# An attention and token-mixing kernel: the one-engine steps up to the first group's end in a written order, and strided heads of two batches on TensorE in small tiles

## The chip, the cores and the metric

The kernel runs on one core of one Trainium2 chip. The metric is the device time of one execution in microseconds, lower is better. It is given as the median of the runs shown; the profile comes from one execution of its own, whose time stands beside its span.

## The reference

The inputs are q, k, v of 8 batches, 8 heads, 576 positions and 64 features, and four weight matrices that arrive in 64-bit floats. Heads 0 to 3 attend to the last 32 positions, heads 4 to 7 to every 32nd position; the result goes through a token-mixing and a channel-mixing layer.

```python
mask_local = (rel >= 0) & (rel < 32)
mask_strided = (rel >= 0) & (pos[None, :] % 32 == pos[:, None] % 32)
scores = np.where(masks, scale * q @ k.T, -1e9)
attn = exp(scores - max); attn = attn / (attn.sum(-1) + 1e-9)
x = (attn @ v) as [batch, 576, 512]
h = np.maximum(x.T @ w_tok1, 0) @ w_tok2      # w_tok1 576 x 256, w_tok2 256 x 576
u = x + h.T
out = u + np.maximum(u @ w_ch1, 0) @ w_ch2    # w_ch1 512 x 1536, w_ch2 1536 x 512
```

## The kernel before

**Groups.** The 8 x 576 = 4608 rows of u are cut into 9 groups of 512. `mlp` handles a group: for each of 12 slices of the hidden layer `up_proj` (12 matmuls of 512 columns, line 460), a relu into gh on ScalarE (463) and the rest gl on VectorE (464), then `down_proj` (12 matmuls, 472) into four accumulators; at the group's end the output is added (486, 488) and stored (489). Every 32-bit factor is split into a high and a low part, which makes three matmuls of one.

**Batches.** Group g needs the u of batch g's main part and of the tail of batch g - 1. For a batch, `load_x` (311) reads x from two arrays in device memory, one of the local heads (xl) and one of the strided heads (xs); `tok1` splits x into xh on ScalarE (327) and xlo on VectorE (328), multiplies (336) and makes h; `tok2` transposes x into PSUM (362), adds the second layer (368), and splits into uh (370, ScalarE) and ul (371, VectorE). These steps are put between the up and down projections of the group before, at places that a table of inserts gives (`at`).

**Attention.** `local_unit` computes two local heads of a pair of batches for n chunks of 128 positions: 8n score matmuls a head pair of 64 by 32 tiles (137), a fused masked minimum on VectorE for each chunk and head (146), an exponential with its sum on ScalarE (149), transposes (160), products with v (167) and a scaling (181). The strided heads of batch 0 go through `strided_pe`: groups of 7 residues, 126 rows, in one matmul (229) with a mask that shuts 6/7 of it, transposes (244) and products (253). The strided heads of batches 1 to 7 go through `strided`: GpSimd multiplies (286, and 303 for the products with v), VectorE sums (287, 305), in 27 + 27 pieces a batch, with buffers sa, sb, and four stores to xs (307).

**Weights.** `convert` turns a raw 64-bit piece (DMA at 85, three raw buffers) into 32 bits in a buffer w_f (two of them): an absolute value on ScalarE (88), a byte copy on ScalarE (92), two steps on VectorE (93, 94). `load_split` then rounds it on ScalarE (105) and takes the rest on GpSimd (106). There are 30 such pieces: 3 of w_tok1, 3 of w_tok2, 24 of w_ch1 and w_ch2. `do_pieces` places the 24 around and inside group 0.

**Order.** Engines take instructions in a queue of their own. The program's text gives priorities, and a planner with times of its own orders each engine's queue from them; `strided` has its work 3000 places later. All DMAs are issued from SP's queue.

Of the kernel before, what the change touches and what calls it, by code (L numbers as in the profile page):

```python
# [10 lines left out]
F32 = mybir.dt.float32  # L11
# [9 lines left out]
HL = 4  # L21
# [10 lines left out]
RG = 7  # L32
RP = RG * NJ
NRG = 5
NSB = 1
FIRST = {0: 1, 4: 2}
# [4 lines left out]
SHUT = -3.0e38  # L41
TOP = 3.4e38
# [11 lines left out]
def attn_mixer_kernel(ctx, tc, qT, kT, vw, qs, ks, vs, qsT, ksT, vsP, mask, mask2, w1, w2, wt1, wt2, outT):  # L54
# [22 lines left out]


    def convert(stage, srcs, n):

# [5 lines left out]
        high = raw[:, :n, 1]  # L86

        nc.scalar.activation(out=a.bitcast(F32), in_=high.bitcast(F32), func=AF.Abs, scale=REBIAS)
# [3 lines left out]
        nc.scalar.copy(out=octets[:, :n, 4], in_=octets[:, :n, 3])  # L92
        nc.vector.tensor_scalar(out=high, in0=high, scalar1=5, scalar2=0x80000007, op0=ALU.arith_shift_right, op1=ALU.bitwise_and)  # L93
        nc.vector.scalar_tensor_tensor(out=a, in0=a, scalar=3, in1=high, op0=ALU.logical_shift_left, op1=ALU.bitwise_xor)  # L94
        return a.bitcast(F32)

    def load_split(stage, dsth, dstl, *srcs):
# [8 lines left out]
        nc.gpsimd.tensor_tensor(out=dstl, in0=f, in1=dsth.bitcast(F32), op=ALU.subtract)  # L106

    def load_t1():
        for c in range(0, NSC - 1, 2):
            load_split(stage, t1h[:, c:c + 2], t1l[:, c:c + 2], *(wt1[P * i:P * i + P] for i in (c, c + 1)))  # L110
# [517 lines left out]
```

## Time and profile before

| | us |
|---|---|
| median of 3 runs | 879.04 (878.23 to 883.42) |
| profiled execution, its own time | 879.49 |
| its span | 877.7 |
| TensorE busy | 836.5 |
| VectorE busy | 482.7 |
| GpSimd busy | 481.3 |
| ScalarE busy | 268.4 |

The mean granted TensorE clock is 0.979. In the profile's rows PE is TensorE, PEld its weight loads, DVE is VectorE, ACT is ScalarE, POOL is GpSimd and SP the engine that issues DMAs. A busy TensorE is not TensorE at its peak: a matmul's end is modelled, so its busy time holds its latency too.

### The profile page before, as it was taken

What the parts mean: (1) busy time and instruction counts of PE and PEld (TensorE: products, weight loads), DVE (VectorE), ACT (ScalarE), POOL (GpSimd) and SP (SyncE); (2) the same over time, 40 slices, a digit from 0 to 9 for tenths busy, and PEclk for the clock granted to TensorE, in tenths of its full rate; (3) what the DMA queues carried; (4) which work ended last, traced back from release to release, by engine and by line L of the source; (5) the groups of instructions that cost most, each with busy time, mean ns of one, the idle gap of its engine ahead of it and who ended that gap; (6) DMA issues with size and microseconds to landing.
All of it is one profiled execution on the core that took longest, in us unless ns stands there. A gap on an engine that the chain in (4) does not pass through costs nothing.

```text
span 877.7 us, 15029 instructions
## 1 busy us (share of the span) xinstructions
PE 836.5 (95%) x5880; PEld 666.5 (76%) x5880; DVE 482.7 (55%) x1171; ACT 268.4 (31%) x738; POOL 481.3 (55%) x453
## 2 busy tenths in 40 slices
PE   6778998899999999999999999999999999999996
PEld 5656776678777788787887887777888877888885
DVE  3999876777377746764665577557622122112112
ACT  5778667141321322122212231213212111111110
POOL 2777976979297849774795779686720002002000
PEclk9959999999998999999999999999999999999999
DMA  9557545150721351044205320521112001001001
GB/s 297 158 166 220 155 149 188 46 174 14 220 86 53 100 166 40 27 132 137 84 0 170 98 90 1 164 88 40 28 49 60 0 1 49 1 1 47 1 1 48
DMA packets 59803, 77.86 MB, mean 89 GB/s; under 512 B 20569, under 2 KB 42073, under 8 KB 59733
## 3 DMA queue, kind: packets, MB, share of 16 engines
q1 hardware_dynamic: 59732, 76.91, 28.4%
q8 instruction: 46, 0.75, 0.4%
q14 instruction: 25, 0.20, 0.1%
HBM read 58.48 MB, written 18.28 MB: 87 GB/s over the span
## 4 chain that ended last, share of the span: by engine, by line
PE 75%; DVE 10%; ACT 5%; DMA 4%; POOL 3%; issue 2%; SPq 1%; DVEq 0%; ACTq 0%; POOLq 0%
PE acc L472 29%; PE h L460 29%; PE t L368 7%; PE t L336 5%; PE t L362 3%; POOL sprod L286 3%; ACT w_raw L92 3%; DVE w_f L94 2%; DVE w_raw L93 2%; DVE xlo L328 1%; PE t L167 1%; PE t L137 1%; DVE ss L287 1%; DMA w_raw<-in_wt 1%; DMA ev<-in_vsP 1%
## 5 line engine op out<-in xcount | busy, mean ns | idle before, releaser
L286 POOL TENSOR_TENSOR sprod<-sb,sa 128x576 f32<-128x576 f32 (+6 forms) x189 | 203.7, 1106 | 94.3 <-DMA sb<-in_ks 64.1
L303 POOL TENSOR_TENSOR sprod<-sa,ss 128x448 f32<-128x448 f32 (+7 forms) x189 | 197.0, 1072 | 42.6 <-DVE ss L296 29.5
L460 PE MATMUL h<-ul,w1h 128*128 128x512 f32 x432 | 170.3, 394 | 1.3 <-DVE ul L371 1.3
L472 PE MATMUL acc<-gh,w2l 128*128 128x512 f32 x432 | 169.4, 392 | 1.3 <-POOL w2l L106 1.3
L460 PE MATMUL h<-uh,w1h 128*128 128x512 f32 x432 | 169.7, 397 | 0.5 <-DVE gl L464 0.5
L460 PE MATMUL h<-uh,w1l 128*128 128x512 f32 x432 | 169.6, 393 | 0.0
L472 PE MATMUL acc<-gl,w2h 128*128 128x512 f32 x432 | 169.5, 392 | 0.0
L472 PE MATMUL acc<-gh,w2h 128*128 128x512 f32 x432 | 165.2, 393 | 1.0 <-ACT w2h L105 0.9
L464 DVE SCALAR_TENSOR_TENSOR gl<-h,gh 128x512 fp32r<-128x512 f32 x108 | 73.7, 686 | 143.9 <-ACT gh L463 143.6
L463 ACT ACTIVATE gh<-h 128x512 fp32r<-128x512 f32 x108 | 64.4, 599 | 280.1 <-PE h L460 274.0
L287 DVE TENSOR_REDUCE ss<-sprod 128x9 f32<-128x576 f32 (+6 forms) x189 | 105.6, 569 | 65.6 <-POOL sprod L286 64.6
L488 POOL TENSOR_TENSOR ot<-ot,ul 128x512 f32<-128x512 f32 x32 | 41.0, 1291 | 174.4 <-DVE ot L486 174.4
L305 DVE TENSOR_REDUCE sb<-sprod 128x64 f32<-128x64 f32 (+8 forms) x189 | 106.3, 569 | 35.9 <-POOL sprod L303 34.5
L460 PEld LDWEIGHTS h<-ul,w1h 128*128 128x128 f32 x432 | 81.3, 188 | 19.1 <-DVE ul L371 2.1
L460 PEld LDWEIGHTS h<-uh,w1h 128*128 128x128 f32 x432 | 81.3, 189 | 18.6 <-DVE gl L464 1.2
L472 PEld LDWEIGHTS acc<-gh,w2l 128*128 128x128 f32 x432 | 81.3, 188 | 18.5 <-POOL w2l L106 2.1
L472 PEld LDWEIGHTS acc<-gh,w2h 128*128 128x128 f32 x432 | 80.9, 188 | 18.5 <-ACT w2h L105 1.7
L472 PEld LDWEIGHTS acc<-gl,w2h 128*128 128x128 f32 x432 | 81.3, 188 | 16.8
L460 PEld LDWEIGHTS h<-uh,w1l 128*128 128x128 f32 x432 | 81.3, 188 | 16.8
L149 ACT ACTIVATE ls<-ls,lm 128x64 f32<-128x64 f32 x144 | 48.1, 335 | 51.5 <-DVE lm L146 51.4
L370 ACT CAST uh<-t 128x512 fp32r<-128x512 f32 (+7 forms) x64 | 25.9, 405 | 111.9 <-PE t L368 111.8
L371 DVE TENSOR_TENSOR ul<-t,uh 128x512 fp32r<-128x512 f32 (+7 forms) x64 | 29.0, 454 | 48.1 <-ACT uh L370 47.8
(80 smaller groups left out, 994.3 us busy)
## 6 DMA issues: line engine op xcount, KB each, us to landing
w_raw<-in_w SPq DMA_DIRECT2D x24, 512.0 KB, 4.2
out_t<-ot SPq DMA_DIRECT2D x36, 256.0 KB, 2.0
x<-xs SPq DMA_DIRECT2D x8, 512.0 KB, 6.4
sa<-in_qs SPq DMA_DIRECT2D x7, 576.0 KB, 3.6
sb<-in_ks SPq DMA_DIRECT2D x7, 576.0 KB, 3.8
sa<-in_vs SPq DMA_DIRECT2D x7, 576.0 KB
xs<-sb SPq DMA_DIRECT2D x28, 144.0 KB, 2.7
lv<-in_vw SPq DMA_DIRECT2D x6, 640.0 KB, 5.4
```

Source lines behind the costliest of these rows:

```text
L149: nc.scalar.activation(out=s_t[:, c, j, :], in_=s_t[:, c, j, :], func=AF.Exp, bias=m_t[:, c, j:j + 1], scale=-1.0, accum_out=z_t[:, c, j:j ...
L286: nc.gpsimd.tensor_tensor(out=pr, in0=k_t[:, n0:n0 + n], in1=q_t[:, i:i + 1].to_broadcast([P, n, D]), op=ALU.mult)
L287: nc.vector.tensor_reduce(out=s_t[:, i, n0:n0 + n], in_=pr, axis=AX.X, op=ALU.add)
L303: nc.gpsimd.tensor_tensor(out=pr, in0=v_t[:, d0:d0 + nd, :n], in1=s_t[:, i:i + 1, :n].to_broadcast([P, nd, n]), op=ALU.mult)
L305: nc.vector.tensor_reduce(out=o_t[:, i, d0:d0 + nd], in_=pr, axis=AX.X, op=ALU.add)
L336: nc.tensor.matmul(ph[m], l, r, start=(c == 0 and k == 0), stop=(short and k == 1))
L368: nc.tensor.matmul(pu[:, :n], l[:, cs], r[:, m, t0:t1], start=False, stop=(m == 1 and k == 2), skip_group_check=True)
L460: nc.tensor.matmul(ph, l[:, cc, fs], r, start=(cc == 0 and k == 0), stop=(cc == NCC - 1 and k == 2))
L463: nc.scalar.activation(out=gh, in_=ph, func=AF.Relu)
L464: nc.vector.scalar_tensor_tensor(out=gl, in0=ph, scalar=0.0, in1=gh.bitcast(F32), op0=ALU.max, op1=ALU.subtract)
L472: nc.tensor.matmul(acc[cc], l[:, fc, cs], r, start=(fc == 0 and k == 0), stop=(fc == NFC - 1 and k == 2))
L488: add.tensor_tensor(out=o_t, in0=o_t, in1=ul.bitcast(F32), op=ALU.add)
```

## The change

**A written order.** The generators of the kernel yield after each piece of work for one engine (a load, the matmuls of a part, one activation, one group of VectorE steps). A string names 398 such steps, 174 up to the input of group 0 and 224 from there to group 1's input, and `in_order` runs them and chains every instruction behind the one before it on its engine, without a semaphore. SP's DMAs are chained too. Steps: S0, S1 and S2, S3 strided heads of batches 0 and 1; L local units of batch 0, M local units of the rest of the first pair; V0 one late unit of batch 2; t, u, w weight pieces (load, ScalarE, VectorE, rounding, rest); X loads of x; Ta, Tb and B tok1; U, Y, C tok2 (batch 0, its tail, batch 1); A, D up and down projections of group 0; G the start of batch 2's strided heads, whose instructions are not chained.

**Strided heads.** `strided_pe` now does batches 0 and 1, four units of two heads: 32 residues x 2 heads of 64 by 32 matmuls, four transposes, and 64 products of 32 by 32 tiles, with v padded to 32 rows and a column of ones for the sum. `strided` begins with batch 2. Its loads stand behind the load of x of the batch before (`issue_after`).

**Local heads.** The softmax works on a whole unit: two masked scalings from PSUM, one minimum, one subtraction, one exponential; the sum comes from a column of ones beside v (65 columns for 64). In the ordered part two PSUM banks are one tile, so that one VectorE instruction reads both.

**Weights.** 13 of the 30 pieces are converted by VectorE alone (no byte copy, three VectorE steps in place of two). The rest is taken by GpSimd for 17 pieces and by VectorE for 13. Pieces no longer run in group 0's inserts, nor does tok1 or tok2 of batch 1.

**Inserts.** One of batch 2's late units moves to insert 26 (group 1), batch 3's move from 28 and 34 to 30 and 36, and the strided heads of batch b from the start of group b - 2 to its place 14.

```diff
+    ON_GPSIMD = "t0 t2 u1 w0 w1 w11 w12 w13 w16 w17 w18 w19 w20 w6 w7 w8 w9"
+    BY_VECTOR = "t2 w10 w12 w13 w14 w15 w16 w17 w2 w21 w4 w6 w9"
...
+        if name in BY_VECTOR.split():
+            yield
+            nc.vector.tensor_scalar(out=a, in0=a, scalar1=3, scalar2=None, op0=ALU.logical_shift_left)
+            nc.vector.scalar_tensor_tensor(out=a, in0=low, scalar=29, in1=a, op0=ALU.logical_shift_right, op1=ALU.bitwise_xor)
+            nc.vector.scalar_tensor_tensor(out=a, in0=high, scalar=0x80000000, in1=a, op0=ALU.bitwise_and, op1=ALU.bitwise_xor)
...
-        nc.gpsimd.tensor_tensor(out=dstl, in0=f, in1=dsth.bitcast(F32), op=ALU.subtract)
+            differ(name).tensor_tensor(out=dstl, in0=f, in1=dsth.bitcast(F32), op=ALU.subtract)
...
-                nc.vector.tensor_tensor_reduce(
-                    out=s_t[:, c, j, :], in0=sc[j][:, 64 * c:64 * c + 64], in1=mask_sb[:, FIRST.get(c0 + c, 0), :],
-                    scale=-SCALE, scalar=TOP, op0=ALU.add, op1=ALU.min, accum_out=m_t[:, c, j:j + 1])
...
+        for j in range(2):
+            nc.vector.scalar_tensor_tensor(
+                out=s_t[:, :n, j, :], in0=sc[j][:, :64 * n].rearrange("p (c k) -> p c k", k=64), scalar=-SCALE, in1=shut,
+                op0=ALU.mult, op1=ALU.add)
+        nc.vector.tensor_reduce(out=m_t[:, :n], in_=s_t[:, :n], axis=AX.X, op=ALU.min)
+        nc.vector.tensor_tensor(
+            out=s_t[:, :n], in0=s_t[:, :n], in1=m_t[:, :n].unsqueeze(3).to_broadcast([P, n, 2, 64]), op=ALU.subtract)
+        yield
+        nc.scalar.activation(out=s_t[:, :n], in_=s_t[:, :n], func=AF.Exp, scale=-1.0)
...
+    def strided_pe(pool, ps_t, b, hp, one=False):
+        qk, v_t = strided_load(pool, b, hp, one)
+        yield
+
+        sc, _ = two_banks(ps_t)
+        for r in range(ST):
+            g, a = divmod(r, 4)
+            for j in range(2):
+                js, rs = slice(64 * j, 64 * j + 64), slice(NJ * r, NJ * r + 32)
+                nc.tensor.matmul(
+                    sc[j][32 * a:32 * a + 32, 32 * g:32 * g + 32], qk[js, rs], qk[js, S + NJ * r:S + NJ * r + 32], start=True, stop=True)
+        yield
...
+            av, banks = two_banks(ps_t)
+            for c in range(4):
+                for a in range(4):
+                    for i in range(2):
+                        ks = slice(32 * (2 * half + i), 32 * (2 * half + i) + NJ)
+                        nc.tensor.matmul(
+                            av[i][32 * a:32 * a + 32, (D + 1) * c:(D + 1) * c + D + 1],
+                            pT[ks, P * c + 32 * a:P * c + 32 * a + 32], v_t[ks, 4 * c + a], start=True, stop=True)
...
+    ORDER = """S0 L0 S1 u2 t0 u1 L1 S0 S0 L0 S0 L0 S0 S0 S0 L0 S0 L0 L0 S0 u2 S1 S0 t0 u2 L0 S0 S1 t1 L2 u2 t0 S1 S1 L0 u0 t0 S1 t0 u2 L1 L0 u1 S1 L1 S1 t1 u1 S1 L2 L1 S1 t2 u1 t1 u1 L1 S1 L1 L2 w1 t1 u0 t1 L1 X0 L3 L1 t2 u0 L1 Ta0 Ta1 L2 Ta0 w4 u0 L2 t2 Ta0 L2 u0 L2 w0 t2 Ta1 Tb0 t2 L2 Ta1 w1 Tb0 L2 L3 Tb0 L3 Tb1 Tb2 Tb1 w4 Tb2 Tb1 L3 w1 L3 Tb3 Tb2 L3 Tb3 w2 w1 L3 w4 Tb3 Tb4 Ta2 Tb4 w0 w3 Ta2 Tb4 L3 Ta2 L3 Tb5 w0 w4 Tb5 w9 w0 w4 Ta3 Ta4 Ta3 w2 Ta4 Ta3 w3 w2 Ta4 Ta5 w3 w5 w2 Ta5 w12 w3 w2 U0 w3 w9 w9 w5 U1 w7 w9 w5 U0 U2 w5 U0 U1 w5 w12 U1 U3 U2 w12 w7 U2 w12 w7 U3 U3 | w1 S3 w0 w9 w16 S3 w6 w12 w10 w7 w7 S3 w16 A0 w6 w16 S3 S3 A0 A1 w6 S3 w8 w16 w16 A0 w11 w6 S3 w6 A1 A2 S3 w10 w8 A1 w10 S3 A2 D0 M1 S3 w20 w10 A3 A2 S3 w10 w8 w11 w13 M1 D1 w8 w11 A3 w8 M1 w17 w11 w11 w20 A4 A3 M1 w20 w13 w14 w20 w13 M1 D2 A4 w20 M1 A4 w19 w17 w13 w17 M1 w13 D3 M0 M1 w21 w17 w14 w17 M1 w14 w19 A5 w19 w15 w14 M0 A5 w14 A6 w22 w19 M0 w19 w21 D4 w21 A6 M0 w15 A5 w23 w21 w15 M0 D5 M0 w21 w18 w15 A6 w22 w15 M0 A7 S2 M0 w23 w22 M0 w22 w23 A8 A7 w22 w23 A7 w18 w23 S2 A9 A8 S2 A8 S2 w18 S2 A10 S2 w18 w18 S2 E V0 D6 S2 S2 A10 D7 S2 A10 S2 V0 A9 D8 A9 V0 O A11 V0 Y3 A11 A11 Y0 Y3 Y3 Y2 Y0 Y0 Y1 Y2 Y2 D9 Y1 X1 Y1 V0 D10 V0 V0 G D11 V0 B V0 B0 B1 B0 B1 B0 B2 B1 B2 B3 B2 B3 B4 B3 B4 B4 B5 B5 C0 C0 C1 C0 C1 C2 C1 C2 C3 C2 C3 C3"""
...
+    def in_order(names):
+        for n in names.split():
+            begun = len(traced)
+            next(steps[n], None)
+            if n != "G":
+                for i in traced[begun:]:
+                    if i.engine in last:
+                        tc.add_manual_dep(i, last[i.engine], mybir.DependencyInfo(mybir.DependencyClass.NoSync, mybir.DependencyReason.DATA), reason="order")
+                    last[i.engine] = i.name
...
     def do_strided(b):
-        strided(sp, b, 3000)
+
+        with tc.issue_after(state["loaded"].ins):
+            strided(sp, b, 3000)
...
-    for b in range(2, B):
-
-        at(HS * (b - 2) if b > 2 else 9, do_strided, b)
-    for b, i0s in enumerate(((17, 22), (28, 34), (44, 54), (68, 78), (92, 102), (116, 126)), 2):
+    for b in range(3, B):
+
+        at(HS * (b - 2) + 14, do_strided, b)
+    for b, i0s in enumerate(((26,), (30, 36), (44, 54), (68, 78), (92, 102), (116, 126)), 2):
```

More of the change, by code (lines that the diff above doesn't have):

```diff
@@ L31 @@
 LC = 5
[L32 to L36, printed above, removed]
+NSB = 2
 NCC = DM // P
@@ L378, in attn_mixer_kernel, with w1_piece @@
     sp = ctx.enter_context(tc.tile_pool(name="sp", bufs=1))
-    def w1_piece(g, c):
+    def w1_piece(name, g, c):
         fs = slice(4 * P * g, 4 * P * g + 4 * P)
-        load_split(stage, w1h[:, c, fs], w1l[:, c, fs], w1[P * c:P * c + P, fs])
-    def w2_piece(c):
-        load_split(stage, w2h[:, c], w2l[:, c], w2[P * c:P * c + P])
-    pieces = [lambda c=c: w1_piece(0, c) for c in range(NCC)]
-    pieces.append(lambda: w2_piece(0))
-    pieces += [lambda c=c: w1_piece(1, c) for c in range(2)] + [lambda: w2_piece(1)]
@@ L391, in attn_mixer_kernel, with w2_piece @@
-    pieces += [lambda c=c: w1_piece(1, c) for c in range(2, NCC)]
+        return split(name, w1h[:, c, fs], w1l[:, c, fs], w1[P * c:P * c + P, fs])
+    def w2_piece(name, c):
+        return split(name, w2h[:, c], w2l[:, c], w2[P * c:P * c + P])
+    pieces = [lambda name, c=c: w1_piece(name, 0, c) for c in range(NCC)]
+    pieces.append(lambda name: w2_piece(name, 0))
+    pieces += [lambda name, c=c: w1_piece(name, 1, c) for c in range(2)] + [lambda name: w2_piece(name, 1)]
+    pieces += [lambda name, c=c: w1_piece(name, 1, c) for c in range(2, NCC)]
@@ L392, in attn_mixer_kernel @@
     for c in range(2, NFC):
[L393 removed]
+        pieces.append(lambda name, c=c: w2_piece(name, c))
         if c < 2 + NCC:
[L395 to L410 removed]
+            pieces.append(lambda name, c=c: w1_piece(name, 2, c - 2))
@@ new lines, in attn_mixer_kernel @@
+    steps = {f"w{k}": p(f"w{k}") for k, p in enumerate(pieces)}
+    traced = nc.cur_bb.bb.instructions
+    last = {}
+    def in_order(names):
[7 more added lines that the diff above has]
+                    last[i.engine] = i.name
@@ L429, in attn_mixer_kernel @@
-        run(*loc[2:], *st)
-        load_x(x_t, 0, 1)
-        tok1(xp, ps_m, x_t, h, slice(0, HL * D))
-        load_t2()
-        us = {0: new_u(xp)}
-        tok2(ps_m, x_t, h, us[0], 0, False, (0, 1))
-        tok1(xp, ps_m, x_t, h, slice(HL * D, DM))
-        tok2(ps_m, x_t, h, us[0], 0, False, (2, 3))
-        do_pieces(4)
-        run(*more[:2])
-        do_pieces(1)
-        run(*more[2:])
+        us = {0: new_u(xp)}
+        for k in range(2):
+            steps[f"S{k}"] = strided_pe(first, ps_w, 0, k)
@@ new lines, in attn_mixer_kernel @@
+        for k in range(4):
+            steps[f"L{k}"] = local_unit(first, ps_w, 0, k % 2, *((0, 3) if k < 2 else (3, 2)), into=x_t)
+        for n, ps in (("t", t1_pieces()), ("u", t2_pieces())):
+            steps.update((f"{n}{k}", p) for k, p in enumerate(ps))
+        for n, cs in (("Ta", slice(0, HL * D)), ("Tb", slice(HL * D, DM))):
+            banks = [ps_m.tile([P, 512], F32, name="t") for _ in range(2)]
+            steps.update((f"{n}{k}", p) for k, p in enumerate(tok1(xp, banks, x_t, h, cs)))
@@ new lines, in later, with once, staging_ends, late @@
+    def later(f, *args):
+        yield from f(*args)
+    def once(f, *args):
+        f(*args)
+        yield
+    def staging_ends():
+        staging.__exit__(None, None, None)
+        pools["late"] = ctx.enter_context(tc.tile_pool(name="late", bufs=1, side="right", reuse_waits="tile"))
+        yield
+    def late(b, hp):
+        return local_unit(pools["late"], ps_t, b // 2, hp, *((5, 4) if b % 2 else (0, 5)), uc=LC)
+    def first_tok1():
+        for k, g in enumerate(get_tok1(1)):
+            steps[f"B{k}"] = g
+        yield
```

450 lines of the change are left out of this document (239 added, 211 removed).

## The prediction

> **What bounds the kernel now.** I read the page first (shares, slices), then busy time by stretches, then the chain of the stretch where the slices look worst.
>
> ```profile
> PE 836.5 (95%) x5880; PEld 666.5 (76%) x5880; DVE 482.7 (55%) x1171; ACT 268.4 (31%) x738; POOL 481.3 (55%) x453
> DVE  3999876777377746764665577557622122112112
> ...
> by line: ACT w_raw L92 15.0%; DVE w_f L94 14.8%; issue 9.8%; DVE w_raw L93 9.3%; PE acc L472 9.1%; DMA x<-xs 5.4%; DVE xlo L328 4.8%; PE t L336 4.5%; ACT w_f L88 4.2%; DVE sb L305 3.9%; PE h L460 2.6%; POOL w1l L106 1.4%; DVE ul L371 1.2%;
> ```
>
> TensorE's 95% is an average. The chain from 60 to 180 us (last row) is not TensorE: the four rows of weight conversion (L88, L92, L93, L94) hold 43% of it, and VectorE is at nine tenths in the first slices. So the beginning is bound by VectorE and the conversions. The stretches:
>
> ```profile
> 0.00:72.00 72.00, 52.91 (x623) 41.53 (x624) 54.16 (x203) 52.18 (x179) 42.74 (x44) 0.86 0.70 216
> 72.00:92.00 20.00, 16.99 (x189) 12.67 (x188) 19.96 (x54) 16.44 (x41) 17.64 (x16) 0.91 0.55 171
> 92.00:178.40 86.40, 78.62 (x372) 60.75 (x373) 63.17 (x104) 48.69 (x75) 68.03 (x57) 0.98 0.42 131
> 178.40:193.00 14.60, 14.49 (x200) 10.78 (x202) 10.73 (x32) 5.57 (x23) 9.74 (x9) 1.00 0.63 192
> 193.00:282.00 89.00, 86.54 (x764) 67.54 (x754) 56.86 (x156) 24.34 (x86) 64.61 (x64) 0.97 0.34 103
> ...
> L371 DVE TENSOR_TENSOR ul<-t,uh x4: 676/676/679, 70.6 to 91.7; 128x512 fp32r<-128x512 f32 x4
> L371 DVE TENSOR_TENSOR ul<-t,uh x4: 614/625/625, 176.7 to 192.4; 128x448 fp32r<-128x448 f32 x4
> L460 PE MATMUL h<-ul,w1h 128*128 128x512 f32 x42 | 16.5, 393 | 0.0
> ...
> 856.00 2.72 PE acc L472 x12
> ```
>
> Columns after the length: TensorE, weight loads, VectorE, ScalarE, GpSimd, clock, DMA. The first L371 row says group 0's input is complete at 92 us; the second that group 1's is at 193. The L460 row is the window 193 to 282: 3 x 42 = 126 of group 1's 144 up-projections are still to come at 193, so 18 are done. A chain row has 12 matmuls in 2.72 us, 0.227 each, so these 18 are 4.1 us ahead: the stage that the order covers ends at an equivalent of **189 us**. What follows is nearly the same work in both kernels.
>
> **The stage in the new kernel: VectorE.** Before, by 193 us it is busy 54.16 + 19.96 + 63.17 + 10.73 = 148 us, of which:
>
> ```profile
> L94 DVE SCALAR_TENSOR_TENSOR w_f<-w_f,w_raw 128x512 uint32<-128x512 uint32 (+2 forms) x30 | 34.3, 1143 | 0.7
> L287 DVE TENSOR_REDUCE ss<-sprod 128x9 f32<-128x576 f32 (+8 forms) x54 | 30.1, 565 | 10.8 <-POOL sprod L286 10.6
> L93 DVE TENSOR_SCALAR w_raw<-w_raw 128x512 uint32<-128x512 uint32 (+2 forms) x30 | 20.4, 681 | 12.7 <-ACT w_raw L92 12.6
> L305 DVE TENSOR_REDUCE sb<-sprod 128x64 f32<-128x64 f32 (+17 forms) x28 | 15.0, 548 | 0.5 <-POOL sprod L303 0.5
> ...
> L93 DVE TENSOR_SCALAR w_raw<-w_raw x30: 389/516/1435, 23.1 to 153.4; 128x512 uint32<-128x512 uint32 x28, 128x256 uint32<-128x256 uint32 x1, 128x128 uint32<-128x128 uint32 x1
> L94 DVE SCALAR_TENSOR_TENSOR w_f<-w_f,w_raw x30: 674/1134/1778, 24.8 to 154.5; 128x512 uint32<-128x512 uint32 x28, 128x256 uint32<-128x256 uint32 x1, 128x128 uint32<-128x128 uint32 x1
> L328 DVE TENSOR_TENSOR xlo<-x,xh x45: 409/823/1884, 28.7 to 702.1; 128x512 fp32r<-128x512 f32 x35, 128x256 fp32r<-128x256 f32 x10
> L106 POOL TENSOR_TENSOR w2l<-w_f,w2h x12: 1267/1282/1723, 72.6 to 156.9; 128x512 fp32r<-128x512 f32 x12
> ...
> L287 DVE TENSOR_REDUCE ss<-sprod 128x9 f32<-128x576 f32 x77 | 57.6, 749 | 35.2 <-POOL sprod L286 34.8
> L287 DVE TENSOR_REDUCE ss<-sprod 128x4 f32<-128x256 f32 x14 | 5.8, 413 | 0.7 <-POOL sprod L286 0.7
> ```
>
> The strided heads of batch 1 (with the start of batch 2's) cost VectorE 30.1 + 15.0 = 45 us; that goes. GpSimd, busy 138 us by 193 (third but last column, summed), keeps 17 splits at 1.28 us, 22 us. With that, prices fall: L94 runs between 0.674 and 1.78 us, and L93 between 0.389 and 1.44.
> - Conversions. 17 in the old form: at the minima 17 x (0.389 + 0.674) = 18.1; 13 on VectorE alone, one shift and two L94-like steps: 13 x (0.389 + 2 x 0.674) = 22.6; together 41 us. At the means (0.681, 1.143): 31 + 39 = 70 us. GpSimd is then busy 22 of some 160 us, not 138 of 193, so I stay near the low end, to which the trace of the new kernel should be nearer: 46.
> - 13 splits moved from GpSimd, two SBUF inputs, 0.68 to 0.93 each: 9. The 15 xlo: 7.5 at their minima.
> - gl, hl and ul, 30 in all at 0.41 to 0.68: 17.
> - Softmax of the new forms, not in the trace. The two L287 forms give 1.05 ns a column plus 0.14 us. A strided unit has 2 steps of 256 columns, 2 of 288, and a normalisation in 6 to 12 small ones: 4.1 us with the wide banks, 5.4 without, 19 for four. Local units by the same rule: 20.
> - Batch 2's strided heads, begun at the end: 5.
>
> Sum 124 us (range 110 to 155). At the fill of before, 148 of 193 or 0.77, that takes **162 us**.
>
> The Trainium skill (SBUF — State Buffer, "Who interferes with whom") says that a VectorE instruction with two SBUF inputs blocks against a GpSimd instruction that reads SBUF, whole instructions long. By it the 13 new conversions and 13 splits are exposed more often than the old ones; if each met GpSimd, the sum would be the means' one, 155 us. The spread 674/1134/1778 of L94 agrees that something stretches it.
>
> **TensorE in that stage.**
>
> ```profile
> 174.09 0.53 PE t L362 x4
> 174.63 1.42 PE t L368 x6
> 176.05 0.69 PE t L137 x40
> ...
> L253 PE MATMUL t<-ev,es 126*126 126x64 f32 (+1 forms) x40 | 9.4, 406 | 1.1 <-ACT es L248 0.7 <-DVE ex L257 0.3
> L229 PE MATMUL t<-ek,eq 64*126 64x126 f32 (+1 forms) x40 | 9.0, 421 | 2.4 <-DVE ss L287 1.3 <-DVE em L232 1.0
> ```
>
> Small tiles are cheap: 40 score matmuls take 0.69 us, with their switch of tile size. A strided unit has 128 of them and four transposes: 2.2 + 0.45 = 2.65 us, 10.6 for four; the old form of batch 0 alone took 18 us of the two last rows. If the 32 by 32 form were as dear as the old one, four units would take 36: 25 more, half of it in the first part, where TensorE is not the bound.
> First part (up to the last U step): VectorE has 10 old and 5 new conversions, 7 splits, two strided and four local units, 10 half-wide xlo and four ul, 50 of the 124. TensorE has 29: 56 half-wide tok1 matmuls (12), tok2 (8), 10 local chunks (4), two strided units (5). ScalarE, 52.18 of 72 before, makes a third fewer byte copies and is no nearer to its limit. At VectorE's fill of the first 92 us, (54.16 + 19.96) / 92 = 0.81, the part ends at **62 us** instead of 92. The half clock of such a thin TensorE (0.86 above) hides there: even 2 x 29 is below 62. Second part, TensorE: 288 x 0.227 = 65.3; two strided units 5.3; 13 local chunks at 0.39, 5.1; batch 0's tail 3.6; tok1 of batch 1 6.7; its tok2 at 0.53 + 1.42, 7.8: sum 94, over VectorE's 75. Waits: 193 to 282 holds 126 + 144 main matmuls (61.2), a tail (3.6), tok1 (6.7) and 13 chunks (5), 76.5 of 89, so 12.5 are lost; I take half, 6, for the second part. 62 + 94 + 6 = **162**, as above.
> Loads: the padded strided operands are some 1.1 MB a unit, 1 MB more in all than the loads that they replace; at the 216 GB/s of the first 72 us that is 5 us of transfer, hidden under engines' work while the share stays at 0.70, and in full if the first unit is what everything waits for.
>
> The Trainium skill (TensorEngine Tiling (Array Packing), "Key Properties") says that changing the tiling mode drains TensorE. Four strided units switch some dozen times more. An estimate: no row isolates a drain, but the 0.69 us above contains one, so by the rule the drains are below 8 us in all, and the stage at most 170 where they are not hidden.
>
> **After the stage.** The 12.5 us lost between 193 and 282 come with this:
>
> ```profile
> L286 POOL TENSOR_TENSOR sprod<-sb,sa x27: 327/1300/1927, 141.1 to 183.7; 128x576 f32<-128x576 f32 x11, 128x64 f32<-128x64 f32 x2, 128x128 f32<-128x128 f32 x2, 128x192 f32<-128x192 f32 x2
> L307 SPq DMA_DIRECT2D xs<-sb x4: 332/458/698, 224.6 to 230.0; - x4
> L314 SPq DMA_DIRECT2D x<-xs x1: 434/434/434, 233.7 to 233.7; - x1
> ...
> L286 POOL TENSOR_TENSOR sprod<-sb,sa x135: 322/1279/1875, 237.2 to 593.6; 128x576 f32<-128x576 f32 x55, 128x64 f32<-128x64 f32 x10, 128x128 f32<-128x128 f32 x10, 128x192 f32<-128x192 f32 x10
> L303 POOL TENSOR_TENSOR sprod<-sa,ss x135: 317/1092/1883, 272.7 to 629.1; 128x320 f32<-128x320 f32 x15, 128x384 f32<-128x384 f32 x15, 128x448 f32<-128x448 f32 x15, 128x512 f32<-128x512 f32 x15
> POOL sprod L286 <- DMA sb<-in_ks: 64.1, 6, 15.4
> ```
>
> Batch 2's strided heads run from 141 to 230 and its x is loaded at 233.7, late in group 1. Later batches take (629.1 + 1.3 - 237.2) / 5 = 78.6 us each, of which 64.1 / 6 = 10.7 are reloading: 68 of work. One of batch 2's two late units leaves group 0 for group 1 (insert 26), so that group 1 has 13 chunks of them as in the old stretch. In the new kernel batch 2's loads stand behind X1, some 26 us of TensorE work ahead of the stage's end; with 7 us of loading the work begins 19 us before that end and is stored 57 after it; x is there 67 after. Group 1 has 65.3 + 3.6 + 5 = 74 us of its own, so 7 us are spare and I count 6 of the 12.5 as saved. Later, loads of batch b also wait in SP's queue behind the x load of batch b - 1 and its stores (some 4 us a batch): 83 against some 88 a group, hidden; without that cover each costs 4. Byte copies, exponentials and read-outs that ScalarE loses lie off the path (123 us busy of 193): nothing.
>
> **Sum.** 877.7 - (189 - 162) - 6 = 844.7 us of span; the profiled run took 879.49, 1.8 more, and lies 0.45 above the median of the runs, 879.04. Forecast: **846 us**.
>
> **Rivals.**
> - *Tighter packing.* VectorE at 0.95 ends the first part near 55 us, TensorE waits for nothing: 150 for the stage, no loss after: about 828. For it: VectorE is full from 72 to 92 (19.96 of 20). Against: long chains of waits.
> - *Strided heads of batch 2 become the bound.* At 92.6 us from first product to x load, as 141.1 to 233.7 shows, plus 6 to land, x is there 80 after the stage's end, 6 too late; a half clock adds some 4: 856. Against: that stretch shared VectorE and GpSimd with conversions.
> - *The fixed order stalls the conversions: slower.* Place: the two w_f buffers, held from L88 to L106. Before, 30 pieces take from 18.8 (first L88) to 158.2, 4.65 us a piece. An engine that waits in a fixed order for one piece has every later step behind it. After the last piece there are 47 us of TensorE work: the stage ends at 15 + 30p + 49. My 162 wants p = 3.3; from 4.35 nothing is gained; at 4.65 it ends at 204 and the time is 888. VectorE's sum at the means' prices, 155 us, gives the same: 155 / 0.77 = 202. Against: 13 pieces lose their byte copy on ScalarE, and GpSimd's strided products no longer stand ahead of the splits.
>
> ```profile
> L88 ACT ACTIVATE w_f<-w_raw x30: 298/674/726, 18.8 to 149.8; 128x512 f32<-128x512 f32 x28, 128x256 f32<-128x256 f32 x1, 128x128 f32<-128x128 f32 x1
> ```
>
> **How the numbers follow.** Forecast band 836 to 860 (stage 152 to 176): 0.50. Tighter, 824 to 836: 0.14. Strided late or part of the stalls, 860 to 870: 0.16. Within 1%, about what a measurement of this kernel can tell from no change, 870 to 888: 0.11. Slower: 0.09. Hence faster 0.80, and a range of 825 to 870 (0.78).
>
> **What would show it.** Right: the first ul quartet ends near 62 us, the one before group 1 near 162, VectorE's L94-like steps mean under 0.9 us, GpSimd idles until about 140, and x of batch 2 comes before group 1's last matmul. Wrong: long waits of ScalarE or VectorE for one piece of weights, TensorE idle between groups 1 and 2, or small-tile matmuls far above 17 ns each.

## The result, and the profile after

The changed kernel takes **886.24 us** (median of 7 runs, 884.49 to 889.32), the kernel before 880.03 (7 runs): a ratio of 1.007 with a 95% interval of 1.0047 to 1.0093 (ratios below have theirs in brackets). It is 0.7% slower; 846, with a range of 825 to 870, was forecast. The profiled span is 886.3 us against 877.7. One execution below, the profiled one of e11, ran at a mean granted clock of 0.847 and is not read.

First the busy time by stretches, as in the prediction's first table; the second fence is the kernel before, up to its own last ul of group 0.

```profile
0.00:73.00 73.00, 44.39 (x1074) 34.98 (x1074) 51.28 (x114) 42.37 (x72) 10.75 (x14) 0.95 0.66 216
73.00:185.00 112.00, 110.04 (x1228) 86.09 (x1221) 71.89 (x156) 46.73 (x78) 32.95 (x29) 0.94 0.50 164
185.00:260.00 75.00, 75.00 (x703) 59.40 (x702) 48.06 (x97) 13.44 (x28) 50.73 (x50) 1.00 0.32 96
260.00:282.00 22.00, 15.24 (x140) 10.24 (x117) 15.12 (x27) 3.53 (x6) 16.74 (x17) 0.77 0.28 91
```

```profile
0.00:92.00 92.00, 69.90 (x810) 54.21 (x810) 74.12 (x256) 68.62 (x219) 60.37 (x60) 0.87 0.66 206
```

Where group 0's and group 1's inputs are complete (one tile's instructions: min/median/max, first and last start):

```profile
L436 DVE TENSOR_TENSOR ul<-t,uh x4: 677/680/684, 65.6 to 72.3; 128x512 fp32r<-128x512 f32 x4
L436 DVE TENSOR_TENSOR ul<-t,uh x4: 625/625/626, 176.6 to 184.3; 128x448 fp32r<-128x448 f32 x4
```

The first part ends at 73 us (before 92, forecast 62), the stage at 185. By then TensorE has run some 15 of group 1's up-projections, so the equivalent is 181.4 (before 189, forecast 162). GpSimd is busy 43.7 us by then, not 138, and VectorE 51.28 + 71.89 = **123.2 us, where 124 was forecast**. So the work is what it was said to be, and the time is not.

To see where the time is, I counted for each TensorE instruction the time from its start to the next one's start. The usual spacing of its form in the later groups (0.227 us for a 512-column matmul) is its work; the rest is TensorE's waiting: idle time, half clock, latency between dependent steps, a slower rate. The rows stop at TensorE's last matmul, 8 us before the span does. In us, with the changed kernel behind the slash:

| stretch | ends at | work | waiting |
|---|---|---|---|
| first part | 92.4 / 73.0 | 51.4 / 31.8 | 37.1 / 35.3 |
| to group 1's input | 193.1 / 184.9 | 84.9 / 94.5 | 15.8 / 17.4 |
| to group 1's output | 275.5 / 259.8 | 76.2 / 70.6 | 6.6 / 4.2 |
| to group 2's output | 375.8 / 376.4 | 90.7 / 97.9 | 9.5 / 18.7 |
| to the end | 877.7 / 886.3 | 480.1 / 481.4 | 13.4 / 20.5 |
| all | | 783.3 / 776.2 | 82.4 / 96.1 |

The first part ends 19 us earlier, and 20 us of TensorE's work left it (half of that went into the next stretch); TensorE waits there nearly as long as before. In all the change takes away 7 us of TensorE's work and adds 14 us of waiting; TensorE also starts at 5.9 us, not 4.0. That is the 8.6 us. (The count depends on the spacing that is taken as usual: with the median of every form, the totals of waiting are 5 to 6 us higher, and the change takes away 6 us of work and adds 12 of waiting.) Group 1 still ends 15.7 us earlier than before, and **between groups 1 and 2 all of it is lost**: 7 us of that are work that stands behind group 1 now, 9 are waiting.

**That boundary**, TensorE's records first (start, length, instruction, idle before it and what ended it), then VectorE's:

```profile
260.53 0.50 PE L536 MATMUL acc<-gh,w2l 128*128 128x512 f32 x1
265.44 0.77 PE L394 MATMUL t<-xh,t1h 128*128 128x512 f32 x1 [4.41 <-DVE lx L230]
266.01 0.63 PE L394 MATMUL t<-xlo,t1h 128*128 128x512 f32 x1
266.43 0.63 PE L394 MATMUL t<-xh,t1l 128*128 128x512 f32 x1
...
273.38 0.50 PE L394 MATMUL t<-xlo,t1h 128*128 128x512 f32 x1 [1.79 <-DVE xlo L385]
```

```profile
261.89 0.22 DVE L215 TENSOR_SCALAR lz<-t 128x4 f32<-128x4 f32 x2
263.36 0.76 DVE L341 TENSOR_REDUCE ss<-sprod 128x9 f32<-128x576 f32 x1 [1.25 <-POOL sprod L340]
264.02 0.19 DVE L216 RECIPROCAL lz<-lz 128x8 f32<-128x8 f32 x1
...
264.88 0.74 DVE L230 TENSOR_TENSOR lx<-t,lz 128x256 f32<-128x256 f32 x2
...
269.52 0.76 DVE L341 TENSOR_REDUCE ss<-sprod 128x9 f32<-128x576 f32 x1 [1.21 <-POOL sprod L340]
270.31 3.62 DVE L385 TENSOR_TENSOR xlo<-x,xh 128x512 fp32r<-128x512 f32 x2
```

x of batch 2 was ready (xh runs from 246.9), but tok1's first matmul needs two PSUM banks that a late local unit of batch 3 holds. Its scaling (lz, lx) stands in VectorE's queue among the group's output additions and the sums of batch 3's strided heads (L341), and each sum waits for a product on GpSimd. TensorE is idle for 4.41 us, then 12 matmuls run 0.43 us apart instead of 0.23, and the next xlo, behind its xh and another sum, takes 1.81 us a piece. The Trainium skill (TensorE: Matmul & The Clock Gate, "Part 1: The HAM clock gate") gives 426.7 ns as the cold spacing of 512 columns and an idle window of about 3.4 us as what brings it; the 0.43 us behind 4.41 us of idleness agrees.

**The rate.** Twelve down-projections in the changed kernel's chain, with nothing waited for:

```profile
701.37 2.79 PE acc L536 x12
```

Before it was 2.72. Those 6 ns a matmul (2.79 and 2.72 us over twelve) were in no term of the sum.

### The profile page after: what moved, and what is told of

Read it like the earlier page. It is cut to its first block, busy times and chain, and to the rows that moved or that the text cites. A ratio compares the mean times of both kernels' runs of the same rounds, so it can differ in the third digit from the quotient of the medians.

```text
span 886.3 us, 16250 instructions
## 1 busy us (share of the span) xinstructions
PE 839.5 (95%) x6820; PEld 664.2 (75%) x6820; DVE 485.8 (55%) x941; ACT 208.4 (24%) x378; POOL 402.3 (45%) x385
## 4 chain that ended last, share of the span: by engine, by line
PE 75%; POOL 9%; DVE 6%; DMA 5%; issue 2%; SPq 2%; ACT 1%; DVEq 0%; POOLq 0%; ACTq 0%
PE h L522 29%; PE acc L536 27%; PE t L431 6%; PE t L394 5%; POOL sprod L340 5%; POOL sprod L357 3%; PE t L425 3%; PE t L170 1%; DVE ss L341 1%; PE t L207 1%; DMA x<-xs 1%; DMA lk<-in_kT 1%; DMA out_t<-ot 1%; DVE xlo L385 1%; PE t L306 1%
## 5 line engine op out<-in xcount | busy, mean ns | idle before, releaser
L340 POOL TENSOR_TENSOR sprod<-sb,sa 128x576 f32<-128x576 f32 (+6 forms) x162 | 173.8, 1102 | 133.9 <-DMA sb<-in_ks 83.0
L357 POOL TENSOR_TENSOR sprod<-sa,ss 128x448 f32<-128x448 f32 (+7 forms) x162 | 162.9, 1035 | 35.5 <-DVE ss L350 25.1
L536 PE MATMUL acc<-gh,w2l 128*128 128x512 f32 x432 | 172.3, 399 | 0.0
L536 PE MATMUL acc<-gl,w2h 128*128 128x512 f32 x432 | 171.5, 397 | 0.0
L536 PE MATMUL acc<-gh,w2h 128*128 128x512 f32 x432 | 168.4, 400 | 0.2 <-ACT gh L526 0.2
L341 DVE TENSOR_REDUCE ss<-sprod 128x9 f32<-128x576 f32 (+6 forms) x162 | 90.6, 570 | 50.1 <-POOL sprod L340 49.1
L359 DVE TENSOR_REDUCE sb<-sprod 128x64 f32<-128x64 f32 (+8 forms) x162 | 91.1, 570 | 35.7 <-POOL sprod L357 34.7
L385 DVE TENSOR_TENSOR xlo<-x,xh 128x512 fp32r<-128x512 f32 (+1 forms) x45 | 39.0, 883 | 31.9 <-ACT xh L382 31.8
```

What stands on the lines that cost most here:

```text
L340: nc.gpsimd.tensor_tensor(out=pr, in0=k_t[:, n0:n0 + n], in1=q_t[:, i:i + 1].to_broadcast([P, n, D]), op=ALU.mult)
L341: nc.vector.tensor_reduce(out=s_t[:, i, n0:n0 + n], in_=pr, axis=AX.X, op=ALU.add)
L357: nc.gpsimd.tensor_tensor(out=pr, in0=v_t[:, d0:d0 + nd, :n], in1=s_t[:, i:i + 1, :n].to_broadcast([P, nd, n]), op=ALU.mult)
L359: nc.vector.tensor_reduce(out=o_t[:, i, d0:d0 + nd], in_=pr, axis=AX.X, op=ALU.add)
L385: nc.vector.tensor_tensor(out=xlo, in0=x, in1=xh.bitcast(F32), op=ALU.subtract)
L536: nc.tensor.matmul(acc[cc], l[:, fc, cs], r, start=(fc == 0 and k == 0), stop=(fc == NFC - 1 and k == 2))
```

## The experiments

The diffs are cut to the lines that matter, and batches are numbered as in the code. "Work" and "waiting" are counted as above, from each run's profile.

**The rate: e1 and e2.** The compiler's layout puts gh and gl at the same place modulo 2048 bytes as w2h and w2l before (896), and 128 bytes off them after (1152 against 1024); the sizes of small tiles changed with the softmax. e1 mends that in the changed kernel; e2 makes the same move before, where it brings the offset.

```diff
-    w1h = const.tile([P, NCC, DF], F32R, name="w1h")
+    sm_sb, w1h = const.tile([P, ST], F32, name="sm"), const.tile([P, NCC, DF], F32R, name="w1h")
```

> The changed kernel with one 128-byte tile (sm) moved from the pool behind the weights to a place in front of them, so that gh and gl lie at the same address modulo 2048 as w2h and w2l, as in the kernel before (in the changed kernel they lie 128 bytes apart). Theory 'addresses': the 432 x 3 down-projection matmuls go from 232.9 to 227 ns apart and the up-projections of the odd groups from 232 to 227, which is 1296 x 6 + 576 x 5 = 8 + 3 us: 886 becomes 875 to 878. Rival 'banks': the accumulators lie in PSUM banks 2 to 5 instead of 0 to 3 and that costs the 6 ns; then nothing changes, 886. Rival 'chip': the profiled run was on another chip; then nothing changes against the changed kernel's own runs.

> The kernel before with the same one-line move, which there puts gh and gl 128 bytes off w2h and w2l modulo 2048. 'Addresses': down-projections go from 226.7 to about 233 ns apart, up-projections of odd groups too: 880 becomes 888 to 891. 'Banks' or 'chip': 880 as before.

e1: 883.71 us, ratio 1.0057 (1.0037 to 1.0078). e2: 887.94, 1.0099 (1.0082 to 1.0117). The same row of e1, then of e2:

```profile
709.00 2.72 PE acc L536 x12
```

```profile
707.46 2.79 PE acc L472 x12
```

The rate goes with the layout in both kernels. Within the changed kernel the up-projections show that it is the distance of the operands and not the place of the weights: those of its group 7, whose uh and ul lie 128 bytes off w1h and w1l, are 232.9 ns apart on the mean, those of group 8, where they lie 1024 bytes off, 228.1. From group 2's output on, e1 takes 495.6 us where the changed kernel takes 501.9; e2 adds 7 us. The whole of e1 gained only 2.5, not the 8 to 11 expected; group 2 ended 2.4 us later in it. The Trainium skill (SBUF — State Buffer, "Who interferes with whom") says that TensorE never waits on anyone for SBUF; these runs show that where its two operands lie matters to it all the same.

**The boundary: e3 to e5, e7.** e3 moves batch 3's and 4's late units out of group 1's end; e5 does so with e1's layout, and e7 in the kernel before. e4 starts batch 2's strided heads before the load of x that they stood behind, 33 us earlier.

```diff
-    ((26,), (30, 36), (44, 54), (68, 78), (92, 102), (116, 126))
+    ((26,), (42, 48), (54, 62), (68, 78), (92, 102), (116, 126))      # e3
+    ((26,), (47, 51), (66, 70), (74, 78), (92, 102), (116, 126))      # e5
+    ((17, 22), (47, 51), (66, 70), (74, 78), (92, 102), (116, 126))   # e7, before
```

> The changed kernel with batch 3's two late local units at inserts 42 and 48 instead of 30 and 36 (batch 4's at 54 and 62), so that none of them holds the two PSUM banks when tok1 of batch 2 could begin. Theory 'late unit': the changed kernel's TensorE stands from 260 to 265 us for the late unit's normalisation, which waits on VectorE behind sums of batch 3's strided heads; then tok1 of batch 2 begins near 250 instead of 265, the half clock from 264 to 278 goes, and 886 becomes 872 to 878. Rival 'strided heads of batch 2 are late': x of batch 2 lands at 247 in both, TensorE stands anyway: 884 to 886.

> The changed kernel with the strided heads of batch 2 started when the buffers come free (behind the score matmuls of unit S2, near 130 us) instead of behind the load of x of batch 1 (153 us). Theory 'late unit': x of batch 2 is there near 225 instead of 247, batch 3's strided heads also run earlier, but tok1 of batch 2 still has to wait for the late unit's banks; a gain below 6 us, 880 to 886. Rival 'strided heads of batch 2 are late': group 2 begins 12 to 18 us earlier, 868 to 875. If the sums disturb the ordered part: its end moves from 185 to 190 or more.

> The changed kernel with the address move of e1 and the late local units put away from every first half of a group: batch 3's at inserts 47 and 51, batch 4's at 66 and 70, batch 5's at 74 and 78 (for 30, 36, 44, 54, 68, 78). Theory 'late unit holds the banks': tok1 of batches 2 and 3 both begin within 3 us of their x; group 2 begins 12 to 15 us earlier than in the changed kernel, as in e3, and group 3 keeps that; with 6 us of e1 after group 2, 886 becomes 862 to 870. Rival 'strided heads set the pace' (a batch of them takes some 88 us from first product to first product, as long as a group): the gain at group 2 is given back by group 4, 878 to 884.

> The kernel before with its late local units at the places of e5 (47, 51, 66, 70, 74, 78 for 28, 34, 44, 54, 68, 78). The theory holds there too: batch 3's first unit stands ahead of tok1 of batch 2 (its normalisation is at 260 us, tok1 begins at 261.6, x was there at 239), so groups 1 and 2 lose less than their 9.2 and 9.5 us: 880 becomes 868 to 875. Rival 'strided heads set the pace': 878 to 882.

All four are slower, and above every range expected: e3 893.06 (1.0165, 1.0143 to 1.0188), e4 893.45 (1.0163, 1.0148 to 1.0179), e5 894.02 (1.0147, 1.0113 to 1.0181), e7 890.54 (1.0097, 1.0065 to 1.0129). e4 settles one point: the results of batch 2's strided heads are stored 32 us earlier (from 204.3 us on, not 236.8), yet the last ul of group 2's input comes at 293.2, as in the changed kernel (293.6). So that rival, whose x comes too late, is not what happens. In e3 and e5 tok1 of batch 2 begins at 247.3 and 249.1 us instead of 265.4, so the late unit is what held it. Group 2 then ends 16 and 24 us earlier, and the lead is lost at a later boundary: in e3 in group 3's interval (102.3 us), in e5 in group 4's (114.5), where four units stand close together. Part of such a lead was never one: in e5 the work up to group 2's output is 287.8 us, not 294.8, because units were put off.

**The written order: e6.** The chain is left off; the planner orders the same program.

```diff
-            if n != "G":
+            if n is None:
```

> The changed kernel without the chain behind each engine's instructions: the same 398 steps are traced in the same order, but the planner orders the queues by its own times. Theory 'the order is worth nothing here': the ordered stage loses as much TensorE time in the changed kernel (47.6 us up to group 0's end) as in the one before (50.3), so the planner does as well: 880 to 890. Rival 'the order packs well and the loss is elsewhere': group 0's end moves from 163 to 172 or more, 893 to 905.

915.59 us, 1.041 (1.0362 to 1.0458). The two stretches of its stage:

```profile
0.00:89.00 89.00, 43.28 (x1114) 33.31 (x1117) 60.87 (x137) 54.11 (x91) 19.49 (x20) 0.95 0.70 235
89.00:215.00 126.00, 112.69 (x1198) 88.23 (x1183) 61.06 (x137) 33.59 (x58) 28.43 (x27) 0.88 0.33 104
```

Without the order group 1's input is complete at 215.3, 22 us later than before the change. So the written order is worth 29 us; without it, the other parts of the change make the kernel 36 us slower than before. What it gains is used up by them. The time is above both ranges expected, and group 0's first output comes at 166.1 us, 3 us later than with the order, not 9 or more: most of the loss lies between there and group 1's input.

**Banks freed by ScalarE: e8.** Layout of e1; ScalarE copies late units' scores and products out of PSUM at once.

```diff
+        if drain:
+            nc.scalar.activation(out=s_t[:, :n, j, :], in_=sc[j]..., func=AF.Copy, scale=-SCALE)
...
+            nc.scalar.copy(out=a_t[:, j0:j1], in_=o[..., :D])
```

> The changed kernel with the shifted addresses of e1 and, for the late local units of batches 3 to 7, ScalarE reading the two PSUM banks (scaled scores; products with v and their sums) into SBUF at once, so that VectorE's masked step and its scaling work from SBUF and no bank waits for VectorE's queue. Theory A (a late unit's VectorE steps, queued behind the sums of the strided heads, hold both banks that tok1 needs): tok1 of batch 2 begins near 249 instead of 265, its last ul comes near 275 instead of 293, group 2 ends near 362 instead of 379, and since the later boundaries are freed too the time is 862 to 872. Theory B (the strided heads' own cycle of loads, products and stores sets the pace from group 2 on, whatever holds the banks): group 2 ends earlier, but the later groups give it back, 878 to 886. Theory C (ScalarE is late too, in its own queue): tok1 of batch 2 stays at 262 or later, 883 to 890.

901.4 us, 1.0237 (1.0198 to 1.0276). TensorE, then VectorE:

```profile
261.36 0.50 PE L408 MATMUL t<-xh,t1h 128*128 128x512 f32 x1
...
271.94 0.80 PE L408 MATMUL t<-xlo,t1h 128*128 128x512 f32 x1 [6.82 <-DVE xlo L399]
```

```profile
265.63 0.75 DVE L355 TENSOR_REDUCE ss<-sprod 128x9 f32<-128x576 f32 x1 [1.44 <-POOL sprod L354]
266.30 2.31 DVE L225 TENSOR_SCALAR lz<-lz 128x8 f32<-128x8 f32 x1
...
269.54 1.75 DVE L244 TENSOR_TENSOR lx<-ls,lz 128x512 f32<-128x512 f32 x1
271.21 0.68 DVE L399 TENSOR_TENSOR xlo<-x,xh 128x512 fp32r<-128x512 f32 x1
```

The bank is free at once (tok1 starts right behind the products), but tok1's next operand, xlo, stands in the same queue: 6.82 us of idleness in place of 4.41. Theory A was half of it, and the time is above the ranges of all three theories. **At this boundary the queue holds TensorE up even where the bank is free.** And steps that read SBUF where they had read PSUM became longer: 2.31 us for 8 columns, while GpSimd runs an output addition and a product. The Trainium skill (SBUF — State Buffer, "Who interferes with whom") says that a VectorE step with two SBUF inputs contends with a GpSimd instruction that reads SBUF, that a scalar step from SBUF to SBUF can contend too, and that the later one then blocks for a whole instruction; this row, and xlo at 1.81, agree.

**Without later strided heads: e9, e10.**

```diff
-        strided(sp, b, 3000)                       # e10; e9 has the same around its two lines
+        if b < 3:
+            strided(sp, b, 3000)
...
-        src = xd[half][b]
+        src = xd[half][min(b, 2) if half else b]
```

> The changed kernel with the shifted addresses of e1, and the strided heads of batches 3 to 7 left out (their x is read from batch 2's result): no products on GpSimd, no sums on VectorE and no loads or stores for them from 250 us on. If these heads and what queues behind them cost the later groups their waits, TensorE works without gaps from group 1's end (260) on: its own work is then some 578 us, so 840 to 850. If not, 875 or more.

> The kernel before with the strided heads of batches 3 to 7 left out in the same way. TensorE's own work from group 1's end (275) on is some 570 us, and its waits there are some 22 us: 850 to 860. Compared with e9: if the earlier stage end of the changed kernel is real and only lost again to the strided heads, e9 is 8 to 15 us faster than this run; if the stage only moved TensorE's work into later groups, the two lie within 4 us.

e9: 868.06 (0.9859, 0.9824 to 0.9893). e10: 874.47 (0.9937, 0.991 to 0.9963). With them gone the changed kernel has 74.4 us of waiting and the old one 77.5, and it is 6.4 us faster, about what the change saves in TensorE's work. That lies between the two expectations (8 to 15, or within 4). Both times were expected too low (840 to 850, 850 to 860). These heads cost the changed kernel 15.7 us (against e1) and the old one 5.6. Without them its lead is 17.6 us at group 1's output (255.4 against 273.0) and still 7.0 at group 2's, where the changed kernel has none left: some of the loss at this boundary is theirs, and some, mostly work put off, is not.

**Places of units and strided heads: e11, e12, e14 to e16.** All have e1's layout but e12, which is the kernel before.

```diff
+    ((26,), (47, 51), (69, 73), (90, 95), (112, 118), (136, 142))     # e11; e12 with (17, 22)
-        at(HS * (b - 2) + 14, do_strided, b)
+        at(HS * (b - 2), do_strided, b)                               # e14: and not behind the x load
+    ((26,), (30, 47), (53, 60), (68, 78), (92, 102), (116, 126))      # e15: e14 and this
+    ((26,), (30, 47), (52, 68), (76, 92), (100, 116), (124, 140))     # e16: e14 and this
```

> The changed kernel with the shifted addresses of e1 and the late local units of all of batches 3 to 7 some 20 inserts later (47, 51; 69, 73; 90, 95; 112, 118; 136, 142), evenly, without the crowding at 66 to 78 that e5 had. If e5 lost its 15 to 23 us of lead only because four units were crowded there, group 4 ends near 537 and the time is 862 to 870. If a later unit only moves the same wait to another boundary, 880 to 892.

> The kernel before with the same later places for the late units of batches 3 to 7. If crowding was e7's fault, 868 to 876, and then the places of these units, not the ordered stage, decide between the kernels. If places later than those of before are worse whatever their spacing, 884 to 892.

> The changed kernel with the shifted addresses of e1, and the strided heads of batches 3 to 7 put where the kernel before has them: at the start of group b - 2, and not behind the load of x of the batch before. Theory (their later start costs the changed kernel the 10 us by which leaving them out helps it more than it helps the kernel before): 871 to 877. Rival (the place doesn't matter, since GpSimd is busy with the batch before until then): 881 to 887.

> e14 with one late unit out of the way of tok1 of batch 2: batch 3's second unit moves from insert 36 to 47, behind that batch's tok1 and tok2, and batch 4's two from 44, 54 to 53, 60. TensorE's waits in group 2's interval, 16 us in e14 against 9 to 10 in the kernel before, fall to 9 or less: 872 to 876, faster than both kernels. If the wait only goes to another boundary or TensorE's work is only postponed, 879 to 885.

> As e15, with the units of every batch from 3 on in the same two places of a group, none across the place of tok1 and tok2 (30, 47; 52, 68; 76, 92; 100, 116; 124, 140). If keeping the units away from tok1 helps at every boundary, 868 to 875; if only group 2's boundary had such a wait, as e15; if later units are worse as such, 885 to 892.

| | us | ratio to before | group 2 ends | work | waiting |
|---|---|---|---|---|---|
| e11 | 889.52 | 1.0095 (1.0063 to 1.0127) | | | |
| e12 | 881.64 | 1.0021 (1.0002 to 1.0039) | 361.9 | 784.8 | 82.2 |
| e14 | 880.32 | 1.0007 (0.9985 to 1.0028) | 369.7 | 778.0 | 86.5 |
| e15 | 884.26 | 1.0057 (1.0037 to 1.0078) | 362.0 | 781.4 | 87.0 |
| e16 | 878.79 | 0.9995 (0.9973 to 1.0017) | 359.5 | 778.0 | 85.9 |

e11 has a time alone. e11 and e12 say that the places alone don't decide: spaced evenly, the old kernel ends group 2 14 us earlier and is still no faster, part of the 14 (4 to 7, by the spacing that is taken as usual) being work put off; crowding was 9 of e7's 10.5 us. e14 gives 3.4 us back against e1, in the direction that its theory said, but not the 7 to 13 that it named. In e16, where no unit runs across tok1, group 2's tok1 starts without a wait while group 1 still runs:

```profile
249.85 0.62 PE L394 MATMUL t<-xh,t1h 128*128 128x512 f32 x2
250.98 0.39 PE L394 MATMUL t<-xlo,t1h 128*128 128x512 f32 x1
```

Waiting up to group 2's output falls from 76.5 us (e1) to 63.4, and with e3 and e5 the boundary's mechanism is thereby shown once more. But behind it the waiting rises from 14.9 to 22.4, and the work put off must still be done. e15, with the old places from batch 5 on, loses its lead in group 3's interval alone (99.6 us, 90.1 in e14). e16 is 7 us faster than the changed kernel, outside each of its three expectations, and not to be told from the kernel before; of the versions that do all the work none is faster than that kernel.

**The first part: e13.** The last VectorE step of 15 weight pieces is left out, 11.7 us.

```diff
+            if name not in FIRST_PART.split():
                 nc.vector.scalar_tensor_tensor(...)
```

> The changed kernel with the shifted addresses of e1 and the last VectorE step of the 15 weight pieces of the first part left out (their values are then not the weights): 11.7 of VectorE's 51.3 us up to 73 us. If the first part is VectorE's work at a constant fill (0.70), its last ul comes 17 us earlier, near 56; if VectorE's work is the bound and its idle time stays (22 us, waits for loads and for TensorE's tiles), 12 us earlier, near 61; if loads and latencies are the bound, under 4 us earlier, 69 or later. As for the whole: if an earlier first part moves the end one for one, 870 to 875; if the later boundaries absorb it, 880 or more.

878.93 us, 0.9992 (0.9972 to 1.0012). Its first ul quartet, and VectorE's stretch:

```profile
L439 DVE TENSOR_TENSOR ul<-t,uh x4: 679/688/694, 64.4 to 69.6; 128x512 fp32r<-128x512 f32 x4
```

```profile
0.00:70.00 70.00, 44.55 (x1077) 35.12 (x1078) 40.24 (x99) 40.96 (x72) 9.24 (x14) 0.95 0.67 223
```

The part ends at 70.3 us. In the ten other traces read here that have the whole of this first part it ends between 71.4 (e3) and 75.2 (e1), at 73.3 on the mean: e13 gains 1 to 5 us, 3 against the mean, for 11.7 us less work. VectorE idles for 29.8 us of the 70, where it was 21.7 of 73. Hence VectorE's work is not what chiefly bound this part. The 4.8 us by which e13's time is below e1's are not this gain carried on: at group 1's input 2.2 us are left of it (182.7 against 184.9), and at group 2's output it is 7.7 (371.1 against 378.8), so most of it arose at the boundary between groups 1 and 2, for a reason that no run isolates.

## Why the prediction was wrong

**The first step that failed is the fill.** "At VectorE's fill of the first 92 us ... 0.81, the part ends at 62 us." This took VectorE as the engine that bounds the part, with idle time in proportion to its work. VectorE's work was right (51.28 us; 50 forecast), and it had 12 idle us in the forecast. It had 17.9 before (92 less 74.12) and has 21.7 now. Held constant, 18 would have given 50 + 18 = 68, still 5 short, and e13 has 29.8 at less work: VectorE was not the chief bound. This step cost 11 us.

What the idle time consists of: VectorE's longest waits up to 73 us (total, times, longest), its longest in the kernel before, and waits of TensorE after the change.

```profile
DVE es L281 <- PE t L275: 8.8, 2, 7.5
DVE em L314 <- PE t L306: 5.0, 3, 1.8
```

```profile
DVE ls L146 <- DMA mask_sb<-in_mask: 8.8, 1, 8.8
```

```profile
PE t L275 <- DMA sa<-in_qksT: 5.9, 1, 5.9
PE t L197 <- ACT ls L190: 3.3, 1, 3.3
PE t L170 <- DMA lk<-in_kT: 3.0, 2, 1.8
PE t L306 <- issue: 2.2, 1, 2.2
PE t L207 <- issue: 1.9, 1, 1.9
PE t L275 <- issue: 1.1, 1, 1.1
```

The wait at the start, 7.5 us for the first scores, is not new: before, VectorE's first step waited 8.8 us. The padded loads that the prediction counted as hidden show in TensorE's start, 5.9 us instead of 4.0.

**The three waits named "issue" are a term that the prediction put at nothing.** They are 5.3 us in which TensorE waits for nothing that the profile shows, at 16.5, 19.5 and 25.1 us, amid the small tiles and on the chain that ended last before 75 us. The five traces of the old form have none. The page of each kernel has a DMA queue that brings instructions, after and then before:

```profile
q8 instruction: 53, 0.87, 0.4%
...
q8 instruction: 46, 0.75, 0.4%
```

TensorE has 13640 matmuls and weight loads after and 11760 before: 256 or 257 for each of these packets in both, so the queue seems to be TensorE's. In all eleven traces of the written order that are read here the waits stand at the same places in TensorE's stream, behind 699, 953 and 1205 instructions, some 254 apart, and end 1.0 to 1.5 us after a packet of this queue has landed; e6, in another order, has the last two as well. So TensorE seems to have run out of instructions. The 128 score matmuls of a strided unit, with their weight loads one packet's worth, take 1.55 us, while packets landed 4 to 6 us apart at that time. The prediction priced a small tile by its 17 ns and asked only for drains. That the part would end 5 us earlier without these waits is not shown; no run changes them.

**The second part's waits.** TensorE's work there, 94 us forecast, is 94.5 with 15 of group 1's up-projections, so 91 without. Its waiting was put at 6 us, half of another stretch's loss, and is 17.4. The old kernel's own value for this stretch was 15.8 and could have been counted. Little of it is idleness (110.04 of the 112 us are busy); part is a mean clock of 0.94 over 112 us, at most 7 us by that figure. With 3 us less of work, this step cost 8 us.

**After the stage.** "7 us are spare and I count 6 of the 12.5 as saved." The condition held: x is there before group 1's end, and e4 shows that it is not late. But x was only one of the things that tok1 needs. The others, two banks and xlo, hang on VectorE's queue, and I had named TensorE idle between groups 1 and 2 as a sign without pricing it. The 6 us were not saved, and the rest of the kernel took 16 us more than before: 7 of waiting up to group 2's output (9 in group 2's row, 2 less in group 1's), 7 of waiting behind it, of which e1 puts 6 down to the matmul rate, and 2 of work. No step had these.

Together 11 + 8 + 6 + 16 is the 41.6 us between the forecast span, 844.7, and 886.3.

**The rivals.** The slower rival gave 888, near the time, by a mechanism that did not occur: the conversions did not stall TensorE, which between 73 and 185 us is idle for 2 us in all. Its nearness is luck. The 30 pieces are converted and split by 131 us, 3.9 us a piece (the forecast needed 3.3, the rival 4.65), and their steps became nearly as cheap as said, 0.73 to 0.82 us against 1.14 before:

```profile
L107 DVE SCALAR_TENSOR_TENSOR w_f<-w_f,w_raw 128x512 uint32<-128x512 uint32 (+1 forms) x17 | 12.3, 725 | 1.1
L98 DVE SCALAR_TENSOR_TENSOR w_f<-w_raw,w_f 128x512 uint32<-128x512 uint32 (+1 forms) x13 | 10.6, 819 | 0.4
L97 DVE SCALAR_TENSOR_TENSOR w_f<-w_raw,w_f 128x512 uint32<-128x512 uint32 (+1 forms) x13 | 9.7, 747 | 0.4
```

The lock's price of 155 us for VectorE's sum did not come about either; GpSimd is busy for only 43.7 us of the stage. Once its instructions are there, a small tile is as cheap as forecast: 64 of the products take 0.79 us between two up-projections, both changes of tile size included (the chain shows 53 of them), so little is left for the 8 us of drains that the prediction allowed for:

```profile
80.80 0.79 PE t L306 x53
```

**What stays open.** Why the waiting that e5, e15 and e16 save at one boundary comes back in later groups. Behind group 2 it is 22.4 us in e16 and 12.9 in e9, without the strided heads of these groups, but e9 has its units in other places. Why e13 loses less at the boundary between groups 1 and 2 than e1. And what of the first part's 11 us belongs to TensorE's instructions, to loads (the chain holds one of local keys from 38.6 to 42.7 us) and to latencies: e13 leaves these three, and no run changed one of them.

## What to carry to other kernels

Ask of the bounding stage whether its idle time shrinks with the work, and list the waits that it consists of: a share of the span is no forecast, and a constant amount isn't one either. A busy engine that loses a fifth of its work may give back little. Many small instructions can cost more than their own time; count them. A stage that ends earlier helps only if everything that the next stage needs moves too: list banks and queue places, not only the data. Check that an edit has not moved the operands of the main loop.

## What the hardware showed

- Matmuls of 512 columns follow each other by 226.7 or 232.9 ns with the place of their two operands in SBUF: 2.72 or 2.79 us for twelve. The slow rate was seen where these lie 128 bytes apart modulo 2048; other small distances were not tried. Moving one tile of 32 columns to another pool changed it (e1, e2), and it is worth 6 to 7 us of a kernel with 2592 such matmuls.
- Where small-tile matmuls follow each other closely, TensorE stood still three times for 1.1 to 2.2 us, some 254 of its instructions apart, each time until 1.4 to 1.5 us after a packet of the instruction queue had landed.
- A step of 8 columns on VectorE took 2.31 us beside GpSimd's output addition and product (e8), and xlo 1.81 instead of 0.68 to 0.69.
